# Linear attention and two MLPs on one core: one step's weight decoding, the numerators' split and the last pair's division are each moved in the order

## The chip, the cores and the metric

One of the eight cores of a Trainium2 chip runs the whole program. The metric is device microseconds from start to end of one execution; lower is better. Five engines work beside each other, each strictly in the order in which its instructions were written: PE (matrix products), DVE (vector), ACT (activations), POOL (general) and SP (issues the DMAs).

## The reference

```python
proj = x @ w_phi;  proj -= max|proj|            # x is q or k: 4 batches, 8 heads, 576 rows, 64 wide
phi  = [exp(proj), exp(-proj)]                  # 256 features
kv   = phi(k)^T v;   z = sum of phi(k)
x    = (phi(q) kv) / (phi(q) z + 1e-6)          # numerator / denominator
...
x = x.reshape(2304, 512)
h = x @ w_in;   x = (h * cos(h)) @ w_out                       # first MLP, 2048 hidden
h = x @ w_in2;  out = (max(h,0) + alpha*min(h,0)) @ w_out2     # second MLP
```

The four MLP weights come as float64 and are needed as the sum of a high and a low part; so each 128x512 tile of them is decoded from its bits on the chip.

## The kernel before, in words

The schedule is written by hand: what a loop issues first, each engine runs first.

**Attention** runs in steps `s` over 40 chunks, eight groups `n` of four heads with five chunks each (the third chunk of a group is short). What a step issues depends on the remainder of `s` by 5, and the list `order` says in which sequence. Per step PE does, in this order: products that build `kv` (L491), one or two numerator products `nm` (L584, `num`; index `y` 0 is copied out of PSUM by DVE and `y` 1 by ACT, both L590), a transpose `tp` of the q scores (L537) and the projections `pj` of the next k and q chunk (L458). DVE takes the maximum off `pj` (L467, L471), then ACT makes the exponentials: `kp` of k (L481), and `qp0h`, `qp1h` of q from `tp` (L556, L570), whose low parts POOL makes (L572). `nm` and `tp` come from one PSUM pool of two buffers, so each new tile waits until the tile before the last has been read.

Behind the numerators of a pair of heads (`n`, `pr`) come, by steps counted from its last product (`after`): `recip` (+2; the denominators go through DRAM by DMA and come back spread over the partitions), `x_mult` (the division, DVE L612) and `x_split` (ACT's `xh`, L619, and POOL's `xl`, L621). These two parts of x are what the first MLP multiplies.

**Weight decoding** of one tile is a chain over three engines: DVE masks and joins (L119, L123, L126, L127), ACT converts (L118, L115, L129), POOL finishes (L132 to L134). In the attention, `w_some` puts its pieces at the end of the steps listed in `W_STEPS`, those with remainders 1, 3 and 4:

```python
W_STEPS = sorted(x + n * NC for n in range(NG4) for x in (6, 8, 9))
W_PARTS = ((0, 0, (0, 1)), (1, 0, (2,)), (2, 0, (3, 5)), (3, 0, (4, 6, 7)), (3, 1, (8, 9)))
```

The four parts carry L119, L123, L126 and L127 on DVE, in this order, one at each step of the list; a tile so takes four places. Five tiles are decoded there.

**The MLPs** run in steps `k` (`moe_step(k)`; the first of them lie in the attention's last steps, `k = s - 48`). PE does `hidden(k + 5)` (`ph`, 12 products), then `output(k)` (`po`, 12 products). In between, DVE and ACT make the gate and `gh`, and POOL makes `gl`; the scratch `r` has two buffers, so `turns` (ACT L183) of a step waits until POOL's `gl` (L86) of two steps earlier has read its `r`. A block of three `ft` for one group of tokens ends with four copies of `po` out of PSUM (L242), which the next `output` waits for. Token groups have 512 tokens, but group 4 has 256: it is the short one. In the first block the groups come as 0, 1, 2, 4, 3, so `hidden` of steps 9 to 11 is short. In the MLP steps all four DVE instructions of a decoding stand together behind `gate`, at the steps `decode_at`, planned from the list `times`.

Of the kernel before, what the change touches and what calls it, by code (L numbers as in the profile page):

```python
# [28 lines left out]
def feature_map_attention_two_mlps(  # L29
# [17 lines left out]
    NG4 = qT.shape[0]  # L47
# [6 lines left out]
    LEAD = 4  # L54
# [112 lines left out]
    def hidden(j):  # L167
        layer, ft, g = steps[j][:3]
        c0, n = groups[g]
        wh, wl = w_t[layer, 0, ft]  # L170
        ph = pools["ps_h"].tile([P, 512], F32, tag="ph", name="ph")[:, 0:n]
        mm3(ph, [
            ((wh[:, kk, :], wl[:, kk, :]), (xh[:, kk, c0:c0 + n], xl[:, kk, c0:c0 + n]))
            for kk in range(KD)
        ])
        h_t[j] = ph

    def turns(j):
        ph = h_t[j]
        r = pools["mt"].tile([P, 512], F32, tag="r", name="r")[:, 0:ph.shape[-1]]  # L180
        h_t[j] = (ph, r)
        if steps[j][0] == 0:
            nc.scalar.activation(  # L183
                out=r.bitcast(I32), in_=ph, func=AF.Copy, scale=1.0 / (2.0 * math.pi)
            )

    def gate(j):
        layer, ft = steps[j][:2]
        ph, r = h_t[j]
        if layer == 0:  # L190
            nc.vector.scalar_tensor_tensor(  # L191
                out=r, in0=r.bitcast(I32), scalar=-2.0 * math.pi, in1=ph, op0=ALU.mult, op1=ALU.add
            )
            nc.scalar.activation(out=r, in_=r, func=AF.Abs)  # L194
            nc.scalar.activation(out=r, in_=r, func=AF.Sin, scale=-1.0, bias=half_pi)
        else:
            nc.vector.tensor_scalar(  # L197
                out=r, in0=ph, scalar1=0.0, scalar2=al[:, ft:ft + 1], op0=ALU.min, op1=ALU.mult
            )

    def activate(j):
        layer, _, g = steps[j][:3]
        n = groups[g][1]
        ph, r = h_t.pop(j)
        gh = pools["gp"].tile([P, 512], F32R, tag="gh", name="gh")[:, 0:n]
        gl = pools["gp"].tile([P, 512], F32R, tag="gl", name="gl")[:, 0:n]
        if layer == 0:
            nc.vector.tensor_tensor(out=r, in0=ph, in1=r, op=ALU.mult)  # L208
        else:
            nc.vector.scalar_tensor_tensor(  # L210
                out=r, in0=ph, scalar=0.0, in1=r, op0=ALU.max, op1=ALU.add
            )
        split(gh, gl, r, nc.gpsimd)
        g_t[j] = (gh, gl)

    def output(j):
# [47 lines left out]
    steps = [  # L264
        (layer, ft, g, fts)
        for x, (layer, fts) in enumerate(blocks)
        for g in (ORDER if 0 < x < len(blocks) - 1 else [0, 1, 2, 4, 3] if x == 0 else range(NG))
        for ft in fts
    ]
# [17 lines left out]
    def quiet(k):  # L287

        return (k < 0 or steps[k][1] != steps[k][3][-1]) and steps[k + LEAD][2] != NG - 1

    decode_at, at, todo = {}, -LEAD - 1, w_all[len(EARLY):]

    times = [t for t in range(2 - LEAD, len(steps) - LEAD) if quiet(t) and not 2 - LEAD < t < 3]
    latest = {}
    for need, free, w in reversed(todo):
        latest[w] = max(t for t in times if t < min([need - 2, *latest.values()]))
# [10 lines left out]
    def moe_step(k):  # L307
        if k in decode_at:
            assert staged[0][:3] == decode_at[k]
            decoding.extend(w_instructions(spare=False))  # L310
            decoding.pop(0)()
        if k < 0:
            hidden(k + LEAD_H)
        elif 0 < k < len(steps) - LEAD_H + 1:
            hidden(k + LEAD_H - 1)
        if k < -LEAD:
            return
        if k + LEAD < len(steps):
            turns(k + LEAD)
        if 0 <= k + LEAD - 1 < len(steps):  # L320
            activate(k + LEAD - 1)
        if k + LEAD < len(steps):
            gate(k + LEAD)
        if len(decoding) == 5:
            while decoding:
                decoding.pop(0)()
        if 0 <= k < len(steps):
            output(k)
        if k in decode_at:
            while len(decoding) > 5:  # L330
                decoding.pop(0)()
            if w_seq:
                fetch_w(*w_seq.pop(0))
        if x_todo:
            split(*x_todo.pop(0))
# [4 lines left out]
    with ExitStack() as actx:  # L340
# [17 lines left out]
        NC = len(chunks)  # L358
# [153 lines left out]
        def kv_some(count=None):  # L512


            while kv_todo and count != 0:
                f, *a = kv_todo.pop(0)
                f(*a)
                count = None if count is None else count - 1
# [115 lines left out]
        )  # L634
        NUM_LAST = 8
        KV_AT, KV_END, KV_LO = {5: (0,)}, {6: (1,)}, {5: (0,), 7: (1,)}
        W_STEPS = sorted(x + n * NC for n in range(NG4) for x in (6, 8, 9))

        def num_step(n, pr, half, y):
            at = next(r for r, x in NUM_AT[y].items() if x == (pr, half))  # L640
            return n * NC + LAG + (at if n < NG4 - 1 else min(at, NUM_LAST))
# [10 lines left out]
        def after(f, d, d_last, *a):  # L652

            def go(s):
                for n in range(NG4):
                    for pr in range(2):
                        if num_step(n, pr, 1, 1) + (d if (n, pr) != (NG4 - 1, 1) else d_last) == s:
                            f(n, pr, *a)
            return go

# [5 lines left out]
        def w_some(s):  # L666
            if not w_run and staged and len(w_t) < len(EARLY) and s in W_STEPS and s >= w_free[0]:
                at = [x for x in W_STEPS if x >= s]
                todo = w_instructions(spare=False)
# [22 lines left out]
        def exp_if(first, half):  # L692

            def go(s):
                if first == any(num_step(n, pr, h, 0) == s for n in range(NG4) for pr in range(2) for h in range(2)):
                    chunk(k_exp, -1, half)(s)
            return go
# [9 lines left out]
            nums_of(1),  # L707
            exp_if(False, 0),
            exp_if(False, 1),
            lambda s: kv_some(),  # L710
            group(kv_lo, KV_LO, 0),
            after(recip, 2, 2),
            after(x_mult, 4, 5),
            chunk(q_transpose, -LAG - 2),
            lambda s: project(s) if s < NK + LAG else None,
            group(kv_hi, KV_END, 0),
# [1 line left out]
            chunk(q_exp, -LAG - 2, 0, True),  # L718
            chunk(q_exp, -LAG - 2, 1, False),
            chunk(q_exp, -LAG - 2, 1, True),  # L720
            after(x_split, 4, 5, False),
            after(x_split, 4, 5, True),
            chunk(less_max, 0, kind="k"),
            w_some,
        )
# [2 lines left out]
        last = (NG4 - 1) * NC  # L728
        S_H = max(NK + LAG, NK + 1, last + max(KV_LO))
        S_O = last + LAG + NUM_LAST  # L730
        NS = S_O + 6
        assert S_H < S_O < S_H + LEAD_H
        for s in range(NS):
            if s + 3 < NK:
                load_x("k", s + 3)
                if s % NC == 2 and s // NC + 1 < NG4:
                    for pr in range(2):
                        load_v(s // NC + 1, pr)
            if 0 <= s - LAG + 3 < NK:
                load_x("q", s - LAG + 3)  # L740
            for stage in order:
                stage(s)
            if s < LAG:

                keep_warm(WARM)
            if s == 5:
                nc.sync.dma_start(
                    out=al, in_=alpha.rearrange("(f p) -> p f", p=P), allow_slow_non_contiguous=True
                )
            if s in (3, 5):  # L750
                fetch_w(*w_seq.pop(0))
            if s == S_H:
                kctx.close()
                pctx.close()
                pools["gp"] = ctx.enter_context(
                    tc.tile_pool(name="gp", bufs=LEAD + 1, reuse_waits="tile", side="right")
                )
                pools["mt"] = ctx.enter_context(
                    tc.tile_pool(name="mt", bufs=2, reuse_waits="tile", side="right")
                )  # L760
                pools["ps_h"] = ctx.enter_context(
                    tc.tile_pool(name="ps_h", bufs=4, space=PSUM, reuse_waits="tile")
                )
            if s == S_O:
                qctx.close()
                w_pools.append(ctx.enter_context(
                    tc.tile_pool(name="wpool2", bufs=1, reuse_waits="tile")
                ))
                w_temps.append(ctx.enter_context(
                    tc.tile_pool(name="wtmp2", bufs=1, reuse_waits="tile")  # L770
                ))
                pools["ps_o"] = ctx.enter_context(
                    tc.tile_pool(name="ps_o", bufs=1, space=PSUM, reuse_waits="tile", side="right")
                )
            if s >= S_H:
                assert not w_run and len(w_t) >= len(EARLY)
                moe_step(s - S_H - LEAD_H)
        assert not nums and not dens

    for k in range(NS - S_H - LEAD_H, len(steps) + 1):  # L780
        moe_step(k)
# [52 lines left out]
```

## Time and profile before

| what | value |
|---|---|
| median of three runs | 1016.78 us (1016.7 to 1017.04) |
| profiled execution, its own time | 1016.79 us |
| its span (first to last instruction) | 1014.4 us, so 2.4 us lie around it |
| PE busy | 990.9 us (98%) |
| DVE, ACT, POOL busy | 719.7, 484.6, 610.0 us |
| mean granted clock of PE | 0.991 of full |

A busy share near 100% on PE means that only PE's waits, and stretches at a lower clock, can be won or added. Times are from the span's start.

### The profile page before, as it was taken

The numbers are of one execution on the slowest core, as the hardware profiler recorded it, in microseconds if no ns is written. First come the engines' busy times: TensorE is split into PE (matmuls) and PEld (weight loads), VectorE is DVE, ScalarE is ACT, GpSimd is POOL, SyncE is SP. The second block draws the span as 40 slices with busy tenths as digits, with TensorE's granted clock in tenths as the row PEclk, the third lists the DMA queues.
The fourth block names the chain that finished last, engine by engine and source line by source line (L and its number), as shares of the span: only waits on it lengthen the run. The fifth ranks groups of instructions, "written<-read, shape, count | busy, mean of one in ns | idle before, by whom it ended". The sixth has DMA issues, their size and how long they took to land.

```text
span 1014.4 us, 14711 instructions
## 1 busy us (share of the span) xinstructions
PE 990.9 (98%) x5515; PEld 829.3 (82%) x5515; DVE 719.7 (71%) x1007; ACT 484.6 (48%) x935; POOL 610.0 (60%) x494
## 2 busy tenths in 40 slices
PE   9999999999999999999999999999999999999998
PEld 6888888787888888888888888888888888888887
DVE  5787898756686795795896778587748774975333
ACT  4777777765665665655666663322212321232000
POOL 1577677656474673573776789756645664576221
PEclk9998999999999999999999999999999999999999
DMA  7254454211020120120111011111101110110112
GB/s 174 79 138 127 110 143 115 63 36 60 30 74 22 42 63 21 43 63 21 63 63 42 21 62 43 42 42 42 62 22 41 49 57 21 42 63 1 42 41 104
DMA packets 64582, 60.67 MB, mean 60 GB/s; under 512 B 28928, under 2 KB 54656, under 8 KB 64512
## 3 DMA queue, kind: packets, MB, share of 16 engines
q1 hardware_dynamic: 64512, 59.75, 19.6%
q8 instruction: 43, 0.70, 0.3%
q14 instruction: 27, 0.22, 0.1%
HBM read 52.50 MB, written 4.79 MB: 56 GB/s over the span
## 4 chain that ended last, share of the span: by engine, by line
PE 82%; DVE 10%; ACT 4%; issue 2%; DMA 1%; POOL 1%; SPq 0%; DVEq 0%; ACTq 0%; POOLq 0%
PE po L164 34%; PE ph L164 34%; PE kv L491 5%; PE nm L584 4%; PE pj L458 3%; DVE wt L123 2%; PE tp L537 2%; DVE wt L126 1%; DVE r L191 1%; DVE we L127 1%; DVE mx L467 1%; PE tp L423 1%; DVE we L119 1%; ACT r L183 1%; ACT r L194 1%
## 5 line engine op out<-in xcount | busy, mean ns | idle before, releaser
L86 POOL TENSOR_TENSOR gl<-r,gh 128x512 fp32r<-128x512 f32 (+1 forms) x160 | 206.8, 1293 | 273.5 <-ACT gh L85 261.0
L85 ACT CAST gh<-r 128x512 fp32r<-128x512 f32 (+1 forms) x160 | 92.0, 575 | 364.1 <-DVE r L210 266.0
L164 PE MATMUL ph<-xh,wil 128*128 128x512 f32 (+1 forms) x640 | 236.8, 370 | 0.1
L164 PE MATMUL ph<-xh,wih 128*128 128x512 f32 (+1 forms) x640 | 236.7, 370 | 0.0
L164 PE MATMUL ph<-xl,wih 128*128 128x512 f32 (+1 forms) x640 | 235.8, 368 | 0.0
L244 DVE TENSOR_TENSOR acc<-po,acc 128x512 f32<-128x512 f32 (+1 forms) x134 | 85.2, 655 | 76.1 <-PE po L164 75.7
L164 PEld LDWEIGHTS ph<-xh,wih 128*128 128x128 f32 x640 | 120.5, 188 | 22.1 <-DVE r L208 0.3
L164 PEld LDWEIGHTS ph<-xl,wih 128*128 128x128 f32 x640 | 120.5, 188 | 22.0
L164 PEld LDWEIGHTS ph<-xh,wil 128*128 128x128 f32 x640 | 120.5, 188 | 21.8 <-POOL wil L134 0.5
L164 PE MATMUL po<-gh,woh 128*128 128x512 f32 (+1 forms) x320 | 119.4, 373 | 3.8 <-ACT r L194 3.3
L164 PE MATMUL po<-gh,wol 128*128 128x512 f32 (+1 forms) x320 | 119.4, 373 | 0.4 <-POOL wol L134 0.4
L164 PE MATMUL po<-gl,woh 128*128 128x512 f32 (+1 forms) x320 | 119.0, 372 | 0.0
L164 PE MATMUL po<-woh,gh 128*128 128x512 f32 x288 | 113.9, 395 | 0.0
L164 PE MATMUL po<-wol,gh 128*128 128x512 f32 x288 | 113.7, 395 | 0.0
L164 PE MATMUL po<-woh,gl 128*128 128x512 f32 x288 | 113.6, 394 | 0.0
L123 DVE SCALAR_TENSOR_TENSOR wt<-ws,we 128x512 int32<-128x512 int32 x64 | 101.7, 1589 | 2.1
L132 POOL TENSOR_TENSOR wu<-wu,we 128x512 f32<-128x512 f32 x64 | 82.9, 1296 | 31.0 <-ACT wu L129 29.1
L197 DVE TENSOR_SCALAR r<-ph,al 128x512 f32<-128x512 f32 (+1 forms) x80 | 55.3, 691 | 58.5 <-PE ph L164 37.8
L126 DVE SCALAR_TENSOR_TENSOR wt<-wu,wt 128x512 f32<-128x512 f32 x64 | 79.1, 1237 | 8.9 <-ACT wu L118 5.4
L491 PEld LDWEIGHTS kv<-vm,kp 128*128 128x128 f32 x512 | 79.0, 199 | 3.8 <-ACT kp L481 3.4
L491 PE MATMUL kv<-vm,kp 128*128 128x66 f32 x512 | 79.8, 262 | 1.8 <-ACT kp L481 1.7
L191 DVE SCALAR_TENSOR_TENSOR r<-r,ph 128x512 f32<-128x512 int32 (+1 forms) x80 | 50.3, 628 | 43.2 <-ACT r L183 41.7
(80 smaller groups left out, 1840.3 us busy)
## 6 DMA issues: line engine op xcount, KB each, us to landing
ws<-in_moe_w_in_dram SPq DMA_DIRECT2D x32, 512.0 KB, 3.7
ws<-in_moe_w_out_dram SPq DMA_DIRECT2D x32, 512.0 KB, 3.5
acc<-dr SPq DMA_DIRECT2D x32, 144.0 KB, 3.0
out_dram<-acc SPq DMA_DIRECT2D x18, 256.0 KB, 2.1
vm<-in_v_dram SPq DMA_DIRECT2D x16, 256.0 KB, 3.6
kin<-in_k_dram SPq DMA_DIRECT2D x28, 128.0 KB, 2.7
qin<-in_q_dram SPq DMA_DIRECT2D x28, 128.0 KB, 3.0
acc<-acc SPq DMA_DIRECT2D x16, 144.0 KB, 2.6
```

The source lines that it names most:

```text
L85: nc.scalar.copy(hi, src)
L86: lo_engine.tensor_tensor(out=lo, in0=src, in1=hi.bitcast(F32), op=ALU.subtract)
L123: lambda: stt(out=t, in0=w1, scalar=-0x40000000, in1=e, op0=ALU.bitwise_and, op1=ALU.bitwise_or),
L126: lambda: stt(out=tf, in0=u, scalar=MIN_PATTERN, in1=tf, op0=ALU.is_ge, op1=ALU.mult),
L132: lambda: tt(out=u, in0=u, in1=ef, op=ALU.mult),
L164: nc.tensor.matmul(ps, lhsT=l, rhs=r, start=(first and m == 0), stop=(last and m == n - 1))
L191: nc.vector.scalar_tensor_tensor(out=r, in0=r.bitcast(I32), scalar=-2.0 * math.pi, in1=ph, op0=ALU.mult, op1=ALU.add)
L197: nc.vector.tensor_scalar(out=r, in0=ph, scalar1=0.0, scalar2=al[:, ft:ft + 1], op0=ALU.min, op1=ALU.mult)
L244: nc.vector.tensor_tensor(out=a, in0=po, in1=a, op=ALU.add)
L458: nc.tensor.matmul(pj[:, j, x, a], lhsT=xt[r, a * P:(a + 1) * P], rhs=w2[r], start=True, stop=True,)
L491: nc.tensor.matmul(kv_ps[pr][:, s, y * VW:(y + 1) * VW], lhsT=e[rows, s, 2 * a + y, :], rhs=v[rows], start=(c == (0, 2)[pr] and a == 0 and ...
L584: nc.tensor.matmul(nm, lhsT=l[:, s, pr, y * VW:(y + 1) * VW], rhs=r[:, s, y, :], start=(s == 0 and m == 0), stop=(s == 1 and m == 2),)
```

## The change

Three places in the order change; no instruction is added or dropped.

- `W_STEPS` has remainders 1, 2, 4 in place of 1, 3, 4. In the MLP steps `times` admits step 7, by which the plan moves one tile, `w_in` of `ft` 4, from `k` = 4 to `k` = 7; no other tile moves.
- `x_split` comes one step later and stands in the middle of that step, ahead of the exponentials of q, where it stood behind them.
- The last pair's `x_mult` stays in its step but goes behind `moe_step(2)`; its `x_split` is one step later, ahead of `moe_step(3)`, and the loop is one step longer (the MLP loop behind it one shorter).

```diff
-    times = [t for t in range(2 - LEAD, len(steps) - LEAD) if quiet(t) and not 2 - LEAD < t < 3]
+
+    times = [t for t in range(2 - LEAD, len(steps) - LEAD) if t == 7 or quiet(t) and not 2 - LEAD < t < 3]
...
-        W_STEPS = sorted(x + n * NC for n in range(NG4) for x in (6, 8, 9))
+        W_STEPS = sorted(x + n * NC for n in range(NG4) for x in (6, 7, 9))
...
-                        if num_step(n, pr, 1, 1) + (d if (n, pr) != (NG4 - 1, 1) else d_last) == s:
+                        d_n = d if (n, pr) != (NG4 - 1, 1) else d_last
+                        if d_n is not None and num_step(n, pr, 1, 1) + d_n == s:
                             f(n, pr, *a)
...
             exp_if(False, 1),
+            after(x_split, 5, 6, False),
+            after(x_split, 5, 6, True),
             lambda s: kv_some(),
             group(kv_lo, KV_LO, 0),
             after(recip, 2, 2),
-            after(x_mult, 4, 5),
+            after(x_mult, 4, None),
...
-            after(x_split, 4, 5, False),
-            after(x_split, 4, 5, True),
...
-        NS = S_O + 6
+        NS = S_O + 7
...
                 moe_step(s - S_H - LEAD_H)
+
+            after(x_mult, None, 5)(s)
```

DVE's queue, end of step 22 (remainder 2), step 23 and the first copy of step 24, before and then after; the line numbers of the changed file are one or two higher.

```order
L467 TENSOR_REDUCE mx<-pj 128x2
L471 TENSOR_TENSOR acc_79<-pj,mx 128x256
L590 COPY acc_80<-nm 65x320
L467 TENSOR_REDUCE mx<-pj 128x4
L471 TENSOR_TENSOR acc_78<-pj,mx 128x512
L600 TENSOR_SCALAR dn<-dn 128x9
L601 RECIPROCAL dn<-dn 128x9
L467 TENSOR_REDUCE mx<-pj 128x4
L471 TENSOR_TENSOR acc_80<-pj,mx 128x512
L123 SCALAR_TENSOR_TENSOR wt<-ws,we 128x512
L590 COPY acc_81<-nm 65x256
```

```order
L468 TENSOR_REDUCE mx<-pj 128x2
L472 TENSOR_TENSOR acc_79<-pj,mx 128x256
L123 SCALAR_TENSOR_TENSOR wt<-ws,we 128x512
L591 COPY acc_80<-nm 65x320
L468 TENSOR_REDUCE mx<-pj 128x4
L472 TENSOR_TENSOR acc_78<-pj,mx 128x512
L601 TENSOR_SCALAR dn<-dn 128x9
L602 RECIPROCAL dn<-dn 128x9
L468 TENSOR_REDUCE mx<-pj 128x4
L472 TENSOR_TENSOR acc_80<-pj,mx 128x512
L591 COPY acc_81<-nm 65x256
```

The decoding's L123 went from ahead of step 24's copy of `nm` to ahead of step 23's.

ACT's queue in the same steps 22 and 23, before and then after.

```order
L570 ACTIVATE qp0h<-tp 128x2x2x128
L619 CAST xh<-acc_81 128x576
L481 ACTIVATE kp<-acc_79 128x256 x2
L590 COPY acc_80<-nm 65x320
L556 ACTIVATE acc_78<-tp 128x512
L570 ACTIVATE qp1h<-tp 128x2x2x128
```

```order
L571 ACTIVATE qp0h<-tp 128x2x2x128
L482 ACTIVATE kp<-acc_79 128x256 x2
L591 COPY acc_80<-nm 65x320
L620 CAST xh<-acc_81 128x576
L557 ACTIVATE acc_78<-tp 128x512
L571 ACTIVATE qp1h<-tp 128x2x2x128
```

The cast of `xh` went from ahead of the copy of `nm` to between it and the exponentials of q.

DVE's queue in the MLP steps 2 to 5 (attention steps 50 to 53), before and then after; the four copies at the top of each piece are those behind `output(2)`.

```order
L612 TENSOR_TENSOR acc_80<-acc_80,acc_82 128x576
L208 TENSOR_TENSOR r<-ph,r 128x512
L191 SCALAR_TENSOR_TENSOR r<-r,ph 128x512
L242 COPY acc_78<-po_2873 128x512
...
L127 TENSOR_SCALAR we<-wt 128x512
L208 TENSOR_TENSOR r<-ph,r 128x512
L191 SCALAR_TENSOR_TENSOR r<-r,ph 128x512
L119 TENSOR_SCALAR we<-ws 128x512
L123 SCALAR_TENSOR_TENSOR wt<-ws,we 128x512
L126 SCALAR_TENSOR_TENSOR wt<-wu,wt 128x512
L127 TENSOR_SCALAR we<-wt 128x512
L208 TENSOR_TENSOR r<-ph,r 128x512
```

```order
L208 TENSOR_TENSOR r<-ph,r 128x512
L191 SCALAR_TENSOR_TENSOR r<-r,ph 128x512
L242 COPY acc_78<-po_2873 128x512
L242 COPY acc_78<-po_2874 128x512
L242 COPY acc_78<-po_2875 128x512
L242 COPY acc_78<-po_2876 128x512
L613 TENSOR_TENSOR acc_80<-acc_80,acc_82 128x576
...
L127 TENSOR_SCALAR we<-wt 128x512
L208 TENSOR_TENSOR r<-ph,r 128x512
L191 SCALAR_TENSOR_TENSOR r<-r,ph 128x512
L208 TENSOR_TENSOR r<-ph,r 128x512
```

The division L612 went from ahead of `output(2)`'s copies to behind them, and the second of two decodings that stood in successive steps is gone from this place.

## Rows read from the trace of the kernel before

**Rows 1.** Busy time by stretch: two stretches, the fourth number from the end PE's clock.

```profile
36.00:199.00 163.00, 148.71 (x1424) 132.99 (x1424) 133.07 (x227) 121.73 (x278) 112.16 (x104) 0.95 0.41 110
262.00:1014.40 752.40, 747.88 (x3497) 619.58 (x3495) 528.92 (x685) 302.59 (x542) 445.57 (x338) 1.00 0.14 45
```

**Rows 2.** PE's waits up to 262 us: sum in us, how many, the longest.

```profile
PE tp L537 <- DVE acc L590: 9.2, 8, 1.6
PE nm L584 <- ACT qp1h L570: 2.2, 8, 0.3
PE kv L491 <- ACT kp L481: 1.7, 3, 0.6
...
PE nm L584 <- ACT acc L590: 1.1, 2, 0.6
```

**Rows 3.** Timeline of PE, steps 24 and 44: start, duration, [idle before].

```profile
110.73 0.33 PE L584 MATMUL nm<-qp0h,kvh 128*66 128x256 f32 x1 [0.28 <-ACT qp1h L570]
...
113.23 0.65 PE L537 MATMUL tp<-ident,acc 128*128 128x128 f32 x4 [1.59 <-DVE acc L590]
...
199.07 0.66 PE L537 MATMUL tp<-ident,acc 128*128 128x128 f32 x4 [0.17 <-DVE acc L590]
```

**Rows 4.** Timeline of DVE, end of step 23 and start of 24.

```profile
111.05 1.79 DVE L123 SCALAR_TENSOR_TENSOR wt<-ws,we 128x512 int32<-128x512 int32 x1
112.76 0.41 DVE L590 COPY acc<-nm 65x256 f32<-65x256 f32 x1
```

**Rows 5.** Timeline of ACT, end of step 22 and step 23.

```profile
105.96 0.69 ACT L619 CAST xh<-acc 128x576 fp32r<-128x576 f32 x1
...
108.11 0.42 ACT L590 COPY acc<-nm 65x320 f32<-65x320 f32 x1 [0.83 <-PE nm L584]
108.61 0.60 ACT L556 ACTIVATE acc<-tp 128x512 f32<-128x512 f32 x1
```

**Rows 6.** Busy time in the four stretches with a low clock.

```profile
40.00:44.00 4.00, 4.00 (x35) 3.78 (x32) 2.01 (x4) 1.61 (x5) 2.50 (x2) 0.57 0.32 95
88.00:95.00 7.00, 7.00 (x50) 6.78 (x49) 2.58 (x5) 3.39 (x7) 5.17 (x5) 0.51 0.61 183
148.00:153.00 5.00, 5.00 (x32) 4.47 (x33) 4.86 (x9) 3.72 (x13) 2.15 (x4) 0.66 0.75 190
187.00:192.00 5.00, 5.00 (x45) 4.78 (x41) 2.34 (x5) 2.29 (x6) 2.49 (x2) 0.66 0.12 36
```

**Rows 7.** Timeline of POOL, DVE and PE in step 23, each from its own list.

```profile
105.20 2.54 POOL L572 TENSOR_TENSOR qp0l<-acc,qp0h 128x512 fp32r<-128x512 f32 x2 [2.37 <-ACT qp0h L570]
...
106.72 0.49 DVE L590 COPY acc<-nm 65x320 f32<-65x320 f32 x1 [0.77 <-PE nm L584]
...
107.91 0.60 PE L537 MATMUL tp<-ident,acc 128*128 128x128 f32 x4
```

**Rows 8.** Timeline of DVE: the same L123 with POOL idle.

```profile
220.63 0.69 DVE L123 SCALAR_TENSOR_TENSOR wt<-ws,we 128x512 int32<-128x512 int32 x1
```

**Rows 9.** Timeline of DVE at step 29's end and of PE in step 31.

```profile
139.75 1.58 DVE L123 SCALAR_TENSOR_TENSOR wt<-ws,we 128x512 int32<-128x512 int32 x1
...
147.66 0.44 PE L491 MATMUL kv<-vm,kp 128*128 128x66 f32 x2 [0.63 <-ACT kp L481]
```

**Rows 10.** Timeline of PE: the starts of `output(3)` and `output(6)`.

```profile
239.94 0.47 PE L164 MATMUL po<-gh,woh 128*128 128x512 f32 x1 [1.71 <-ACT r L194]
...
254.44 0.47 PE L164 MATMUL po<-gh,woh 128*128 128x512 f32 x1 [1.59 <-ACT r L194]
```

**Rows 11.** Timeline of DVE and of ACT ahead of these two starts.

```profile
236.51 0.76 DVE L612 TENSOR_TENSOR acc<-acc,acc 128x576 f32<-128x576 f32 x1 [1.95 <-DMA acc<-dr]
...
239.11 2.48 DVE L242 COPY acc<-po 128x512 f32<-128x512 f32 x4
...
253.62 2.47 DVE L242 COPY acc<-po 128x512 f32<-128x512 f32 x4
...
233.24 0.60 ACT L183 ACTIVATE r<-ph 128x512 int32<-128x512 f32 x1 [2.71 <-POOL gl L86]
```

## The prediction

> **What bounds the kernel now.** I first read busy time by stretch. From 262 us on PE is busy for 747.88 of 752.40 us at full clock [rows 1]; nothing is moved there, and I leave it at its length. The change works between 36 and 262 us. From 36 to 199 us PE stands still for 163.00 - 148.71 = 14.3 us, and its granted clock is 0.95 in the mean [rows 1]. So two things can be won: waits, and clock.
>
> Next, PE's waits. The largest is that of the transposes `tp` for DVE's copy of `nm` (L590): 9.2 us in eight waits [rows 2]. They come five steps apart, in steps of remainder 4; seven have a decoding instruction of the step before ahead of the copy. The rows of step 24 show it: DVE runs L123 for 1.79 us from 111.05 and starts the copy only at 112.76, without an idle gap between, and `tp` starts at 113.23 after 1.59 us of waiting [rows 3, 4]. The eighth, step 44, has no decoding ahead and waits 0.17 us [rows 3]. So seven waits, 9.2 - 0.2 = 9.0 us, hang on the instruction that W_STEPS moves. In the same steps PE waits another 0.28 us for ACT's exponentials of the step before, as these free the PSUM buffer of `nm` with `y` 1 [rows 2, 3].
>
> Third, the clock by stretch. [...] What that costs is length times missing clock: 4 x 0.43 + 7 x 0.49 + 5 x 0.34 + 5 x 0.34 = 8.55 us, if all of PE's work there goes with the clock. Three of the four follow a wait of the kind above; the third follows waits for `kp` [rows 9].
>
> Last, the start of the MLP: `output(3)` waits 1.71 us and `output(6)` 1.59 us [rows 10].
>
> **The change, part by part.**
>
> *Decoding off remainder 3.* It takes the 9.0 us of waits away as far as DVE is concerned: without L123 the copy of step 24 could start at about 111.05, and `tp` is not ready for it before 113.23 - 1.59 = 111.64. What is late next is ACT, by the second edit.
>
> *The split one step later.* On ACT the cast (0.69 us) goes from ahead of the copy that ends at 108.53 to behind it; the exponentials that began at 108.61 come later by between 0.08 less than the cast, 0.61 us, and nothing [rows 5]. ACT waited 0.83 us for PE ahead of that copy, so taking the cast away in front gains nothing [rows 5]. Since instructions of one engine overlap a little I take 0.5 us. All of it lands on PE, for the wait of 0.28 us in rows 3 is a wait for these exponentials. Seven groups: 7 x 0.5 = 3.5 us given back. **Term 1: -9.0 + 3.5 = -5.5 us** (bounds -9.0 and -4.7).
>
> *Decoding onto remainder 2.* Three L123 and two L126 now stand ahead of the copy of steps with remainder 3. In step 23 DVE is free from 106.72 - 0.77 = 105.95; with the 1.79 us of rows 4 the copy starts at 107.74, ends at 108.23, and `tp`, which started at 107.91, waits 0.32 us [rows 4, 7]. With L123's 0.69 us beside an idle POOL [rows 8] it would wait for nothing. POOL is at its `qp0l` pair then, from 105.20 for 2.54 us [rows 7], so the long value is nearer. **Term 2: 3 x 0.32 = +1.0 us** (bounds 0 and, with the two L126 at the same price, +1.6).
>
> The row shows L123 at 1.79 us with POOL at work and 0.69 us without. [...]
>
> *Remainder 1.* In steps 16, 31 and 36 PE waits for `kp` and for ACT's copy, 1.7 + 1.1 = 2.8 us in all [rows 2, 9]. Ahead of two of them, L123 (1.58 us, rows 9) gives way to the first mask L119; behind them L123 comes in for L126; ahead of the third, and of step 21, an L127 comes in that stood a step earlier. These go against each other. **Term 3: 0** (bounds -2.8 and, two L123 in full, +3.2).
>
> *Clock.* The waits after which it fell shrink from 0.28 + 1.59 to some 0.28 + 0.5 us, but those of remainder 1 stay. I take three of the short stretches as gone, 5.1 of 8.55 us. **Term 4: -5.1 us** (bounds -8.55 and 0).
>
> *Last pair, and the decoding of k = 4.* DVE stands 1.95 us for the DMA of the denominators and 0.76 us in L612 ahead of the copies that `output(3)` needs, which start at 239.11 (rows 10 name ACT's L194 as what ended the wait, but the first of these copies ends last) [rows 11]. Behind the copies this is 2.7 us they don't wait, more than the 1.71. What is late next is the scratch `r`: ACT already waits 2.71 us for `gl` [rows 11], and the other pair's `xl` (estimate 1.4 us: half of the `qp0l` pair, 576 columns for 512) now stands ahead of that `gl`. I leave 0.5 us. Then `xl` of the last pair must be there for the short `hidden(9)`: copies to about 240.5, L612 to 241.2, cast to 241.9, `xl` to 243.3 [rows 5, 7, 11]; `output(3)` begins at 238.2 + 0.5 and takes 12 products of 0.21 us [rows 1], so `hidden(9)` begins about 241.3 and asks for its fourth quarter of `xl` a good microsecond later: 0.7 us of waiting. SP's queue is not passed: the same DMAs in the same order, so the landing time stands. The second wait, of `output(6)`, is for copies that start at 253.62 [rows 11] behind two decodings in successive steps; one of them, at least 1.6 us on DVE by its L123 alone [rows 9], goes to k = 7, where the next copies wait for PE anyway. I take it as gone. **Term 5: -(1.71 + 1.59) + 0.5 + 0.7 = -2.1 us** (bounds -3.3 and 0).
>
> Sum: -5.5 + 1.0 + 0 - 5.1 - 2.1 = -11.7 us. The profiled execution took 1016.79 us, as the median of 1016.78; forecast **1005.1 us**.
>
> **The rivals.** *The clock doesn't come back.* The same four stretches, or others as long: -6.6 us, 1010.2 us. For it: they follow small waits, of which some remain. Against: after the wait of 1.59 us in rows 3 it didn't fall at all. [...]
>
> *More comes back.* The cast hides (-3.5 more) and the clock is whole (-3.4 more): 998.2 us. For it: 0.83 us of idle time on ACT just ahead [rows 5]; against: that idle time lies on the wrong side of the cast.
>
> *The wait only moves.* Term 2 at 1.6 us, Term 3 at 3.2, Term 4 and 5 at nothing: about 1016 us, no change. For it: DVE is busy for 133 of 163 us [rows 1]; against: the 0.77 us of idle time in rows 7.
>
> *Slower: the clock falls in every group.* A fall costs 8.55 / 4 = 2.1 us. Terms 1, 2, 3 and 5 give 6.6 us, or 3.1 falls; so from eight falls on, in place of four, it is slower, about 1018.7 us. For it: the wait for ACT in steps of remainder 4 grows from 0.28 to 0.8 us in all seven groups. Against: each is less than half of what stood there.
>
> **How the numbers follow.** Forecast 0.58 (own range 1000.5 to 1008.5), clock not back 0.21, more back 0.08, wait moved 0.07, slower 0.06. A run tells a difference from 0.2%, that is 2.0 us. The first three are faster: 0.87; same 0.07; slower 0.06. Range 1000.5 to 1013, which leaves out the last two, the upper edge of the second and most of the third.
>
> **What would show it.** Right: `tp` no longer waits for L590 in steps of remainder 4, and the wait of `nm` for `qp1h` is 0.7 to 0.9 us in their place; the copies of remainder 3 follow a decoding directly; one or two stretches below full clock from 36 to 199 us; `output(6)` starts without a wait. Wrong: a new wait of `tp` in steps of remainder 3 near a microsecond, L590 waiting for `xl` of the pair three earlier (whose buffer it writes), or the clock low after the waits for ACT.

## The result and the profile after

The changed kernel takes 999.6 us (median of four runs, 999.39 to 1000.1), the kernel before in the same session 1016.91 us (1016.7 to 1019.2): ratio 0.9825, 95% interval 0.9808 to 0.9842. It is faster by 17.3 us where 11.7 were forecast, and 0.9 us below the low end of the range. The profiled execution took 999.44 us, with a span of 997.7 us against 1014.4. Lines have moved by one or two: L591 is the copy of `nm`, L538 the transposes `tp`, L571 and L573 the high and low parts of q's exponentials, L620 the cast, L622 `xl`.

PE's waits after, which answer to [rows 2, 10] (sum, times, longest):

```profile
PE nm L585 <- ACT qp1h L571: 5.1, 8, 0.8
PE tp L538 <- DVE acc L591: 3.3, 4, 1.1
...
PE ph L164 <- POOL wil L134: 1.0, 1, 1.0
...
PE po L164 <- ACT r L194: 0.4, 1, 0.4
...
PE ph L164 <- POOL xl L622: 0.4, 1, 0.4
PE kv L492 <- ACT kp L482: 0.2, 1, 0.2
```

`tp` went from 9.2 to 3.3 us, `kp` from 1.7 to 0.2, ACT's copy from 1.1 to nothing. `nm` for `qp1h` more than doubled, and waits for `wil` and `xl` are new. Busy time by stretch, to set beside [rows 1, 6] (the fourth number from the end is the granted clock):

```profile
36.00:186.00 150.00, 141.56 (x1437) 127.18 (x1436) 123.89 (x229) 123.51 (x281) 117.85 (x108) 1.00 0.45 123
186.00:997.70 811.70, 804.94 (x3776) 667.00 (x3774) 562.56 (x741) 340.02 (x610) 484.39 (x367) 1.00 0.14 45
```

The clock is 1.00 throughout. The timeline of PE in step 24, beside [rows 3]:

```profile
102.72 0.34 PE L585 MATMUL nm<-qp0h,kvh 128*66 128x256 f32 x1 [0.65 <-ACT qp1h L571]
103.48 0.60 PE L538 MATMUL tp<-ident,acc 128*128 128x128 f32 x4
```

The 1.59 us of `tp` are gone, and the 0.28 us of `nm` have become 0.65. DVE in steps 23 and 24, beside [rows 4, 7]:

```profile
97.88 0.98 DVE L123 SCALAR_TENSOR_TENSOR wt<-ws,we 128x512 int32<-128x512 int32 x1
98.78 0.47 DVE L591 COPY acc<-nm 65x320 f32<-65x320 f32 x1
...
102.67 0.41 DVE L591 COPY acc<-nm 65x256 f32<-65x256 f32 x1
```

The decoding now stands ahead of the copy of remainder 3, as forecast, but takes 0.98 us there, not 1.79. ACT in step 23, beside [rows 5]:

```profile
99.73 0.42 ACT L591 COPY acc<-nm 65x320 f32<-65x320 f32 x1 [1.00 <-PE nm L585]
100.05 0.67 ACT L620 CAST xh<-acc 128x576 fp32r<-128x576 f32 x1
100.62 0.59 ACT L557 ACTIVATE acc<-tp 128x512 f32<-128x512 f32 x1
```

The cast stands between the copy and the exponentials. PE's wait of 0.65 us is for these exponentials, which the cast has made later.

### The profile page after: what moved, and what is told of

Read it like the earlier page. It is cut to its first block, busy times and chain, and to the rows that moved or that the text cites. A ratio compares the mean times of both kernels' runs of the same rounds, so it can differ in the third digit from the quotient of the medians.

```text
span 997.7 us, 14697 instructions
## 1 busy us (share of the span) xinstructions
PE 981.0 (98%) x5515; PEld 821.1 (82%) x5515; DVE 708.5 (71%) x1007; ACT 484.1 (49%) x935; POOL 614.2 (62%) x494
## 4 chain that ended last, share of the span: by engine, by line
PE 82%; DVE 8%; ACT 5%; POOL 3%; issue 3%; DMA 0%; POOLq 0%; ACTq 0%; DVEq 0%
PE po L164 36%; PE ph L164 34%; PE kv L492 4%; PE nm L585 3%; PE pj L459 2%; DVE wt L126 2%; PE tp L538 1%; POOL xl L622 1%; DVE wt L123 1%; PE tp L424 1%; DVE mx L468 1%; ACT acc L557 1%; DVE r L191 1%; DVE we L119 1%; ACT qp1h L571 1%
## 5 line engine op out<-in xcount | busy, mean ns | idle before, releaser
L123 DVE SCALAR_TENSOR_TENSOR wt<-ws,we 128x512 int32<-128x512 int32 x64 | 95.5, 1492 | 2.1
L126 DVE SCALAR_TENSOR_TENSOR wt<-wu,wt 128x512 f32<-128x512 f32 x64 | 81.2, 1269 | 8.5 <-ACT wu L118 4.9
L492 PE MATMUL kv<-vm,kp 128*128 128x66 f32 x512 | 76.2, 255 | 0.3 <-ACT kp L482 0.2
L492 PEld LDWEIGHTS kv<-vm,kp 128*128 128x128 f32 x512 | 74.9, 190 | 2.0 <-ACT kp L482 1.5
## 6 DMA issues: line engine op xcount, KB each, us to landing
acc<-dr SPq DMA_DIRECT2D x32, 144.0 KB, 3.0
acc<-acc SPq DMA_DIRECT2D x16, 144.0 KB, 2.8
```

The source lines that it names most:

```text
L123: lambda: stt(out=t, in0=w1, scalar=-0x40000000, in1=e, op0=ALU.bitwise_and, op1=ALU.bitwise_or),
L126: lambda: stt(out=tf, in0=u, scalar=MIN_PATTERN, in1=tf, op0=ALU.is_ge, op1=ALU.mult),
L492: nc.tensor.matmul(kv_ps[pr][:, s, y * VW:(y + 1) * VW], lhsT=e[rows, s, 2 * a + y, :], rhs=v[rows], start=(c == (0, 2)[pr] and a == 0 and ...
```

## The experiments

The kernels of one group ran on one chip, beside runs of the kernel before, and each group on another chip; the medians of before are 1018.81 us for the first group, 1017.87 for the second, 1019.01 for the third. These runs of before reach from 1015.92 to 1022.12 us, so ratios carry wide intervals; versions of one group are compared by their medians. The change itself took 999.6 us at first and 999.76 in the second group, which says how far medians of different groups can be compared.

### Each part alone (first group)

Only the table entry:

```diff
-        W_STEPS = sorted(x + n * NC for n in range(NG4) for x in (6, 8, 9))
+        W_STEPS = sorted(x + n * NC for n in range(NG4) for x in (6, 7, 9))
```

> The kernel before with only the decoding's steps changed (remainders 1, 2, 4). Theory A, the clock falls because PE waits: the 9.0 us of waits of the transposes for DVE's copy shrink to under 1.5, the wait for ACT's exponentials stays at 2.2, and with the waits go the three low stretches behind them (6.9 us of 8.55); the one near 150 us may stay. About 1002 us. Theory B, the low clock has another cause and came back by the other edits or by chance: the same waits go, the low stretches stay: about 1009 us.

Measured: 999.81 us (999.59 to 1000.19), ratio 0.9811 [0.9791, 0.9831]. The entry alone is as fast as the whole change. Theory A holds by its waits and by the clock: no low stretch is left in the attention, and the time is 2 us below the one that it gave. PE's waits with it:

```profile
PE nm L584 <- ACT qp1h L570: 2.6, 8, 0.6
PE po L164 <- ACT r L194: 2.1, 1, 2.1
PE tp L537 <- DVE acc L590: 1.6, 5, 0.5
```

The wait of 2.1 us is that of `output(3)`; behind it the clock is 0.57 for 4 us:

```profile
223.29 0.48 PE L164 MATMUL po<-gh,woh 128*128 128x512 f32 x1 [2.10 <-ACT r L194]
```

```profile
224.00:228.00 4.00, 4.00 (x14) 3.17 (x13) 3.97 (x6) 2.95 (x5) 1.39 (x2) 0.57 0.00 0
```

Only the splits moved:

```diff
+            after(x_split, 5, 6, False),
+            after(x_split, 5, 6, True),
             lambda s: kv_some(),
...
-            after(x_split, 4, 5, False),
-            after(x_split, 4, 5, True),
```

> The kernel before with only the numerators' split one step later, in the step's middle. Theory A: the wait of nm for ACT grows by about 0.4 us in each of seven groups, but the transposes behind it wait for DVE's copy anyway, so that wait shrinks by as much; the 1.1 us of nm waiting for ACT's copy go; clock as before. 1015 to 1017 us. Rival: the later exponentials are paid in full, 2.9 us: about 1019.8 us.

Measured: 1011.42 us (1011.29 to 1011.44), ratio 0.9924 [0.9904, 0.9944]. `tp` falls to 5.5 us and `nm` rises to 6.7. Both expected times were missed: it is 7.4 us faster than before on the same chip. The waits in the attention shrink by little, from 14.2 to 13.3 us; what both left out is the clock, 0.997 in all four runs where before has 0.983 to 0.993. In the attention one low stretch is left, a mean clock of 0.57 from 40 to 44 us, behind the one `tp` that still waits 1.58 us; the others wait 0.90 us at most.

Only the last pair's product behind the output step, its splits one step later:

```diff
-            after(x_mult, 4, 5),
+            after(x_mult, 4, None),
...
-            after(x_split, 4, 5, False),
-            after(x_split, 4, 5, True),
+            after(x_split, 4, 6, False),
+            after(x_split, 4, 6, True),
...
                 moe_step(s - S_H - LEAD_H)
+            after(x_mult, None, 5)(s)
```

> The kernel before with only the last pair changed: its division behind the output step, its split one step later. By the trace after, the wait of 1.71 us becomes about 0.8 us in two places; attention and clock as before. About 1016.0 us; if the second wait (1.59 us, behind two decodings) shrinks too because the copies are earlier, 1014.5 us; if it grows by what the first loses, 1016.9 us.

Measured: 1020.17 us (1013.66 to 1022.59, ten runs), ratio 1.0004 [0.9984, 1.0024]: nothing that can be told, and the three expected times lie closer together than its runs. The two waits of [rows 10] merge into one of 3.05 us, and behind it the clock falls as well (0.72 in the mean from 248 to 254 us).

Only step 7 admitted:

```diff
-    times = [t for t in range(2 - LEAD, len(steps) - LEAD) if quiet(t) and not 2 - LEAD < t < 3]
+    times = [t for t in range(2 - LEAD, len(steps) - LEAD) if t == 7 or quiet(t) and not 2 - LEAD < t < 3]
```

> The kernel before with only the one decoding moved from step 4 to step 7. The second wait (1.59 us) goes, the first (1.71 us) stays, and PE waits about 1 us for the weights of a later decoding, as in the trace after: about 1016.3 us. Rival: with DVE later by the first wait there is no such new wait: 1015.3 us.

Measured: 1015.0 us (1010.12 to 1018.42, ten runs), ratio 0.9956 [0.9934, 0.9979]. By its waits the rival holds: `output(6)` no longer waits, `output(3)` still waits 1.7 us, and no wait for weights is new. The time, with runs 8 us apart, can't tell the two.

These last two price the clock, because every run comes with its mean granted clock. The step-7 version had two runs at 1.000, of 1010.12 and 1010.22 us, and its two slowest at 0.986, of 1018.42 and 1018.24 us: the same instructions, 8.2 us apart. 0.014 of a span of 1016 us is 14.2 us of missing clock, so a microsecond of it costs about 0.58 us (0.54 to 0.62, as the clocks are given to 0.001). The version with only the last pair's edit was profiled in its fastest run. Its stretch in the attention, with the clock at 1.00, and its first wait of `tp`:

```profile
36.00:194.00 158.00, 142.69 (x1428) 126.21 (x1426) 136.62 (x227) 121.75 (x278) 112.80 (x103) 1.00 0.42 114
```

```profile
39.15 0.55 PE L537 MATMUL tp<-ident,acc 128*128 128x128 f32 x3 [1.57 <-DVE acc L590]
```

It has before's waits in the attention, 9.2 us of `tp`, without a low clock behind them. So it is the kernel before at full clock, as far as the attention goes.

### The change again, and a wait put back (second group)

> The changed kernel itself, as the measure for the runs beside it: 999.6 us within half a microsecond.

Measured: 999.76 us (999.26 to 1002.04), ratio 0.9825 [0.9804, 0.9845].

Then five in-place multiplications of a spare tile on VectorE at the end of each remainder-3 step from 8 to 38, which nothing reads:

```diff
+            if s % NC == 3 and 8 <= s < 40:
+                for _ in range(5):
+                    nc.vector.tensor_scalar(out=spare_t, in0=spare_t, scalar1=1.0, scalar2=None, op0=ALU.mult)
```

> The changed kernel with five idle DVE instructions on a spare tile (0.42 us each) at the end of the steps of remainder 3, where the decoding stood; the decoding itself stays where the change put it. They make the transposes of seven steps wait again, 1 to 1.5 us each, 7 to 10 us in all. Theory A, the clock falls because PE waits: one to four low stretches come back at random, so 1010 to 1018 us, and runs of the same kernel spread over several microseconds. Theory B, the low clock belonged to the decoding or to something else: only the waits, 1007 to 1010 us, runs within one microsecond.

Measured: 1022.69 us (1020.37 to 1023.0), ratio 1.0046 [1.0035, 1.0058]. Both theories missed the time. One multiplication took 0.97 us in the mean where 0.42 was taken, and the largest waits are of `nm` for DVE's copy (10.0 us in six, the longest 3.50), not of `tp`: too much, and in another place, so it doesn't decide between the two for `tp`'s waits of 1.6 us. Behind the longest the clock was 0.62 from 144 to 152 us, behind the next, of 2.99 us, 0.57 from 68 to 76 us; behind two waits of 1.49 us it stayed at 1.00.

The first pair's splits back behind the exponentials, the second pair's left in the middle:

```diff
-            after(x_split, 5, 6, False),
-            after(x_split, 5, 6, True),
+            after(x_split, 5, 6, False, 1),
+            after(x_split, 5, 6, True, 1),
...
+            after(x_split, 4, 6, False, 0),
+            after(x_split, 4, 6, True, 0),
             chunk(less_max, 0, kind="k"),
...
+            if pr != of:
+                return
```

> The changed kernel, but the split of a group's first pair is back in the division's step behind the exponentials; the second pair's stays where the change put it. If the cast ahead of the exponentials is what makes nm wait for ACT, that wait falls from 5.1 to 2.2 us and the 1.0 us of transposes in steps 14 and 29 shrink too: 995.5 to 997 us. Rival: the cast behind the exponentials makes kp late instead: no gain, 999.6 us.

Measured: 996.86 us (996.11 to 997.26), ratio 0.9791 [0.9774, 0.9808]; 2.9 us faster than the change on the same chip. `tp` waits for DVE 0.2 us in all, as expected; `nm` waits for `qp1h` 3.5 us, not the 2.2 expected.

The same with POOL's last two instructions of a tile a step later and the extra decoding at step 6:

```diff
-        W_PARTS = ((0, 0, (0, 1)), (1, 0, (2,)), (2, 0, (3, 5)), (3, 0, (4, 6, 7)), (3, 1, (8, 9)))
+        W_PARTS = ((0, 0, (0, 1)), (1, 0, (2,)), (2, 0, (3, 5)), (3, 0, (4, 6, 7)), (3, 2, (8, 9)))
...
-    times = [t for t in range(2 - LEAD, len(steps) - LEAD) if t == 7 or quiet(t) and not 2 - LEAD < t < 3]
+    times = [t for t in range(2 - LEAD, len(steps) - LEAD) if t == 6 or quiet(t) and not 2 - LEAD < t < 3]
```

> As the kernel before this one, and the last two POOL instructions of a decoding one step later (behind the split), and the one MLP decoding at step 6 in place of 7. If the copies of steps 22 and 37 wait for a split that stands behind these two POOL instructions, 2.3 us of waits go; and the wait for weights (1.0 us) goes with step 6: 992.5 to 994 us. Rival: POOL's two instructions delay the low parts of q in their new place, and step 6 brings the wait for the copies back: 996 us.

Measured: 1009.59 us (1008.2 to 1009.98), ratio 0.9914 [0.9896, 0.9933]. Both expected times were missed: it is 12.7 us slower than the version that it starts from. There are two waits of `nm` for ACT's copy, each followed by a stretch at a mean clock of 0.57 to 0.58. The first wait, and what stood ahead of the copy on ACT:

```profile
100.45 0.53 PE L585 MATMUL nm<-qp1h,kvh 128*66 128x320 f32 x1 [4.23 <-ACT acc L591]
```

```profile
98.43 0.68 ACT L118 ACTIVATE wu<-ws 128x512 f32<-128x512 f32 x1 [4.83 <-POOL wil L134]
```

The two POOL instructions, now later, hold up the next tile's L118 on ACT, and with it the exponentials of k and the copy behind.

### Which part counts beside the others (third group)

The change with the old entry:

```diff
-        W_STEPS = sorted(x + n * NC for n in range(NG4) for x in (6, 7, 9))
+        W_STEPS = sorted(x + n * NC for n in range(NG4) for x in (6, 8, 9))
```

> The changed kernel with the one table entry put back (decoding slots 6, 8, 9 of each tile instead of 6, 7, 9). Theory (the table entry carries nearly all of the gain: 199.07 to 182.08 us for the last q transposition in the run of the entry alone): the waits of tp at remainder 4 are back (5 to 6 us in sum, eight of them), the last q transposition stands at 192.5 to 193.5 us, the end is 10 to 12.5 us above the changed kernel, 1010 to 1012.5 us. Rival (the moved splits or the last pair's edits carry part of it by themselves): below 1007 us, tp waits below 3 us.

Measured: 1009.37 us (1009.07 to 1011.94), ratio 0.9915 [0.9891, 0.994]. The theory holds by its waits (`tp` 5.4 us) and nearly by its time: it is 1009.37 - 999.76 = 9.6 us slower than the change, on another chip.

The splits of both pairs back:

```diff
-            after(x_split, 5, 6, False),
-            after(x_split, 5, 6, True),
...
+            after(x_split, 4, 6, False),
+            after(x_split, 4, 6, True),
             chunk(less_max, 0, kind="k"),
```

> The changed kernel with the splits of both pairs put back behind the exponentials (last pair's edits, table entry and step 7 kept). If the parts add up: 999.8 us of the table entry alone, less 0.9 us after the attention, 998.9 us; the changed kernel lies 0.7 to 1.2 us above it (the moved splits as a whole cost about 1 us), and the version with only the first pair's put back 2 us below it (the second pair's move is a gain). Rival (only the first pair's place matters, the second pair's is free): 996.5 to 997.2 us. Second rival (the moved splits are a gain that the table entry alone lacks): above 1000.5 us.

Measured: 997.53 us (996.54 to 997.81), ratio 0.9792 [0.977, 0.9815]. My theory falls: the parts didn't add up to 998.9. Beside the new entry the moved splits as a whole cost 999.76 - 997.53 = 2.2 us; the place of the second pair's is worth at most 997.53 - 996.86 = 0.7 us, with ranges that overlap. From the entry alone, 999.81, to this kernel, 997.53, the last pair's edits and step 7 gain 2.3 us. These three differences are each between two chips. In the change the first and the last cancel.

The first pair's splits back, with step 6 for step 7:

> The version with the first pair's splits put back behind the exponentials (996.86 us), with the extra decoding at step 6 of the output chain instead of step 7. Theory (PE's wait of 0.99 us for wil is the decoding of step 7 standing against that of step 9 on POOL): the wait falls below 0.3 us, the time by 0.5 to 1.0 us, 995.9 to 996.4 us. Rival (the low part is late for another reason and the wait turns up elsewhere): within 0.3 us of 996.9.

Measured: 996.05 us (995.82 to 996.31), ratio 0.9779 [0.9757, 0.9801], the lowest median of all. As expected PE waits less for `wil`:

```profile
PE ph L164 <- POOL wil L134: 0.2, 1, 0.2
```

And a wait put back with reductions in place of multiplications, in the version with only the first pair's splits back:

```diff
+            if s % NC == 3 and 8 <= s < 40:
+                for _ in range(3):
+                    nc.vector.tensor_reduce(out=spare_m, in_=spare_t, axis=AX.X, op=ALU.max)
```

> The version with the first pair's splits put back, with three extra reductions over 512 values on VectorE (a spare tile, nothing reads the result) at the end of each of the eight remainder-3 steps from 11 to 39, in the place that the decoding left. Estimate for one, from the reductions and subtractions of 512 values in the trace: 0.5 to 0.8 us, 1.5 to 2.4 us in all. Theory (a wait of 1.1 to 1.8 us of TensorE can bring the granted clock down to 0.5 for some us behind it, in some executions): waits of about 1 to 2 us at eight steps in place of the present 0.2 us in sum, low-clock stretches behind some of them, runs that spread over more than 2 us, time 1006 to 1014 us. Rival (the waits cost only themselves, and the low clock of the kernel before came from elsewhere): the same waits, clock 1.00 throughout, runs within 1 us, 997 us plus the waits' sum.

(The steps are the seven of remainder 3 from 8 to 38.) Measured: 1004.24 us (1003.48 to 1004.72), ratio 0.9859 [0.9836, 0.9881]. Its waits of `tp`, and the attention's stretch:

```profile
PE tp L538 <- ACT acc L591: 7.7, 7, 1.2
PE nm L585 <- ACT qp1h L571: 2.5, 8, 0.6
PE tp L538 <- DVE acc L591: 2.3, 3, 1.1
```

```profile
36.00:188.00 152.00, 139.60 (x1421) 124.91 (x1422) 136.77 (x245) 121.50 (x276) 114.81 (x102) 1.00 0.44 118
```

These 10.0 us of waits of `tp`, of up to 1.2 us each, are in sum about as much as before's 9.2, and bring no low clock in the profiled execution: 7.4 us slower (than the other group's 996.86), runs within 1.3 us. The rival holds for waits of this length: of the four runs three have a mean clock of 1.000 and one of 0.997.

## Why the prediction fell short

Two marks of PE's timeline split the span: the transposes of step 8 (33.45 us before) and those at 199.07 us [rows 3], 165.62 us apart before. The second are those of step 42, not of step 44 as the rows and the prediction call them: step `s` transposes chunk `s` - 4, so the short third chunk of a group, two transposes in a row of the timeline, falls on remainder 1. In the same way PE's waits for `kp` lie in steps 17, 32 and 37, not 16, 31 and 36. No sum hangs on these numbers. The same marks in the change, 150.54 us apart:

```profile
32.92 0.60 PE L538 MATMUL tp<-ident,acc 128*128 128x128 f32 x4
...
183.46 0.66 PE L538 MATMUL tp<-ident,acc 128*128 128x128 f32 x4
```

with the last pair's edit alone, which is before's attention at full clock, 160.42 us:

```profile
33.84 0.60 PE L537 MATMUL tp<-ident,acc 128*128 128x128 f32 x4
...
194.26 0.66 PE L537 MATMUL tp<-ident,acc 128*128 128x128 f32 x4 [0.16 <-DVE acc L590]
```

and with the table entry alone, 148.73 us:

```profile
33.35 0.60 PE L537 MATMUL tp<-ident,acc 128*128 128x128 f32 x4
...
182.08 0.66 PE L537 MATMUL tp<-ident,acc 128*128 128x128 f32 x4 [0.16 <-DVE acc L590]
```

The version with the splits of both pairs back has 32.89 and 181.64, 148.75 us: the other edits don't touch the attention.

| part of the span | forecast, us | measured, us |
|---|---|---|
| clock (Term 4) | -5.1 | 160.42 - 165.62 = -5.2 |
| table entry at full clock (Terms 1 to 3 without the cast) | -9.0 + 1.0 + 0 = -8.0 | 148.73 - 160.42 = -11.7 |
| the splits, in the attention (Term 1's cast) | +3.5 | 150.54 - 148.75 = +1.8 |
| behind step 42 (Term 5) | -2.1 | (997.7 - 183.46) - (1014.4 - 199.07) = -1.1 |
| ahead of step 8 (32.65 to 33.84 us over all versions, old entry or new) | 0 | 32.92 - 33.45 = -0.5 |
| sum | -11.7 | -16.7 |

The time that lies around the span fell as well, from 2.4 to 1.7 us, which makes up the 17.3 us; no term had it, and why it fell isn't shown.

**The step that failed is the sum of Terms 1 to 3**: -4.5 us by forecast, -9.9 by the marks. Four sizes in it were wrong, all to the same side but the first: -8.5, 0, -2.1 and +1.8 us, and about -1 more in rows that count as busy.

*Term 1 without the cast* held nearly: of the 9.0 us of `tp` for DVE's copy in seven steps, two waits of 0.27 us are left, -8.5 us.

*Term 2* is 0 where +1.0 was taken. No `tp` waits in the steps of remainder 3 with the entry alone, nor after. I priced L123 by the row of step 23's end, 1.79 us beside POOL's `qp1l` pair, and carried that price to a place beside the `qp0l` pair. All L123 of the attention, first before, then after (min, median and max in ns):

```profile
L123 DVE SCALAR_TENSOR_TENSOR wt<-ws,we x5: 1576/1779/1789, 36.6 to 183.7; 128x512 int32<-128x512 int32 x5
```

```profile
L123 DVE SCALAR_TENSOR_TENSOR wt<-ws,we x4: 729/854/978, 70.6 to 165.3; 128x512 int32<-128x512 int32 x4
```

After has a fifth ahead of the row's four: it begins at 30.66 us, 0.40 us into a pair of POOL's subtractions, and lasts 1.43 us. In step 23, too, POOL is at such a pair in the old place as in the new one, but L123 comes at another moment of it. Before, it begins at 111.05 [rows 4], when the first half of the first pair below has just ended, and lasts until behind the pair's end; after, it begins at 97.88, 1.06 us into the second pair below, and has ended at 98.86:

```profile
109.77 2.52 POOL L572 TENSOR_TENSOR qp1l<-acc,qp1h 128x512 fp32r<-128x512 f32 x2 [0.67 <-ACT qp1h L570]
```

```profile
96.82 3.19 POOL L573 TENSOR_TENSOR qp0l<-acc,qp0h 128x512 fp32r<-128x512 f32 x2 [0.77 <-ACT qp0h L571]
```

It takes 0.98 us there where it takes 0.69 beside an idle POOL [rows 8], and the pair takes 3.19 us where it took 2.54 in the same step before [rows 7]. So both engines pay, POOL now the larger part (0.65 us, DVE 0.29), and the price of L123 belongs to its place. To go by the row's 1.79 us was the mistake. Of the 11.2 us by which VectorE's busy time falls (719.7 to 708.5, 1007 instructions in both) L123 makes 6.2; POOL's rises from 610.0 to 614.2.

*Term 3* is -2.1 us where I took 0. With the entry alone the waits for `kp` fall from 2.4 us (in the full-clock run of before's attention) to 0.5 and those for ACT's copy from 1.1 to 0, against two new waits of `tp` of 0.45 us: -1.9 - 1.1 + 0.9. I had let L123, L126 and L127 cancel one another, L123 at the 1.58 us of [rows 9].

*The cast* costs 1.8 us in the attention where I took 3.5. The forecast wait is there: `nm` for `qp1h` at 0.6 to 0.8 us in seven steps, 5.1 us in sum where the entry alone has 2.6. Only six of the seven grew; step 42 has its 0.62 us in the entry alone too. What I named as a wrong sign is there as well, copies that wait for an `xl`, here in step 29, with `tp` behind them (DVE, PE and POOL, each from its own list):

```profile
125.88 0.42 DVE L591 COPY acc<-nm 65x256 f32<-65x256 f32 x1 [1.15 <-POOL xl L622]
```

```profile
126.35 0.66 PE L538 MATMUL tp<-ident,acc 128*128 128x128 f32 x4 [0.75 <-DVE acc L591]
```

```profile
121.83 1.27 POOL L133 TENSOR_TENSOR wt<-wt,wih 128x512 f32<-128x512 f32 x1
123.18 1.28 POOL L134 TENSOR_TENSOR wil<-wt,wu 128x512 fp32r<-128x512 f32 x1
124.42 1.42 POOL L622 TENSOR_TENSOR xl<-acc,xh 128x576 fp32r<-128x576 f32 x1
```

Measured from one `tp` to the next, the steps that end with the `tp` of steps 14, 19, 29 and 34 are 0.74, 0.34, 1.25 and 0.31 us longer than with the entry alone, and all others together 0.8 us shorter. With the first pair's splits back these four last as long as with the entry alone (3.6 to 3.8 us). So the cost is the first pair's.

The longest waits, 1.14 and 1.13 us of `tp` in steps 22 and 37, cost next to nothing. From the `tp` of step 21 to that of 22 it takes 5.54 us, and 5.50 with the entry alone, where `tp` waits 0.45. There the products ahead are spread out instead, which I put down to `kv` waiting for `kp`: the rows of two `kv` products that start at 90.53 and 91.06 us take 0.44 us each, those behind them 0.33. One product's row is 0.31 to 0.34 us long there and the next row starts 0.14 to 0.18 us behind its start, so a delay of that size shows as busy time. Between the marks PE is therefore idle for 3.9 us more than with the entry alone, but busy for 2.1 us less (141.8 against 144.0).

The last 1.0 us of the table's -11.7 lies in such rows too, as the idle time fell by 10.7 us: the stretches that end with the `tp` of steps 17 and 32, where `kv` waited for `kp`, lost 0.7 us each beyond their idle time.

*Term 4* had the right size, by luck in its halves. I took the three short stretches at their full 8.55 - 3.4 us, though one of them follows waits for `kp` that I let stand. All four went, and a microsecond of missing clock is worth about 0.58: 8.55 x 0.58 = 5.0. The 8.55 us, the lengths of the stretches of [rows 6] times their missing clock, stood on all of PE's work there going with the clock, and the runs don't show that: between the marks, from before to the last pair's edit alone, PE's busy time falls by 6.3 us (151.25 to 144.96), and its waits grow by 1.1. The first rival didn't come about: 8.6 us of waits, each up to 1.1 us, stand between products after, and the clock stays at 1.00. The second rival, which gave 998.2 us a chance of 0.08, came nearest: the clock is whole, as it says, but the cast isn't hidden, and Terms 2 and 3, which it left as they were, make up for that.

*Term 5* is right in its places and 1 us short in the span. Timeline of PE:

```profile
222.94 0.47 PE L164 MATMUL po<-gh,woh 128*128 128x512 f32 x1 [0.43 <-ACT r L194]
227.52 0.38 PE L164 MATMUL ph<-xl,wih 128*128 128x256 f32 x1 [0.37 <-POOL xl L622]
...
264.39 0.49 PE L164 MATMUL ph<-xh,wil 128*128 128x512 f32 x1 [0.99 <-POOL wil L134]
```

`output(3)` waits 0.43 us (forecast 0.5), `hidden(9)` 0.37 for `xl` (forecast 0.7), `output(6)` starts without a wait. What I left out is the third row: the decoding put at k = 7 stands on POOL next to that of k = 9. Moving it to step 6 takes the 0.99 us to 0.2 and gives 996.86 - 996.05 = 0.8 us, between two chips and with ranges that overlap by 0.2 us. With the splits alike, the edits of this term gain 2.3 us (entry alone against both pairs back) and 1011.42 - 1009.37 = 2.0 us (splits alone against the change with the old entry), again between chips. That this is near the 2.1 us of the forecast is luck: of the 2.4 us by which the stretches behind step 42 differ in the first of these pairs (816.0 against 813.7), only 0.9 are waits. The other 1.5 us are busy time, and the entry alone has the low clock shown above, behind its wait of 2.10 us, which the kernel before doesn't have there. The splits alone likewise have a mean clock of 0.57 from 248 to 252 us, behind a wait of 1.77.

## What to carry to other kernels

Price an instruction that is moved by what it will meet in its new place, and when, not by its longest row: here L123 took 1.58 to 1.79 us in its old places of the attention and 0.73 to 1.43 in the new ones, though POOL subtracts beside it in both, and so Terms 2 and 3 erred to the same side. Take the edits apart even when the whole is faster: one number in a table is enough for all of the gain, and beside it a second edit, which alone had gained 7.4 us, cost 2.2 us and hid a third that gained as much. Where runs of one program spread, put each run's granted clock beside its time before any of them is explained.

## What was not expected of the hardware

The spread of the kernel before (1015.92 to 1022.12 us) goes with the granted clock of each run (0.993 to 0.983). The entry alone, without the waits of 1.6 us in the attention, lies within 0.6 us; but so do the splits alone, within 0.15 us, though one wait of 1.58 us is left there, with a low clock behind it in the profiled execution. Before's attention waits, the first of them 1.58 us, had a low clock behind them in the profiled execution of before (0.57 from 40 to 44 us behind the first) and none in the one shown above, where the first is 1.57 us, with the same instructions around them. Nine waits of `tp` in the version with reductions, 1.1 us in the mean and 1.2 at most, had none behind them in the profiled run; yet in the trace of before a low stretch followed waits of about 0.6 us [rows 6, 9]. The six waits of 2.10 to 4.23 us that the traces have were all followed by a low clock, 0.57 to 0.62 in the mean of 4 to 8 us, and 0.72 from 248 to 254 us behind the one of 3.05. For the shorter ones length alone doesn't decide it, and what does stays open.
